# A fused retention and gated feed-forward kernel: a new order for its first sixteen microseconds, and one GpSimd product moved ahead of a hold

## The chip, the core and the metric

The kernel runs on one core of one Trainium2 chip. The metric is the device time of one execution in microseconds (us). Six executions of the kernel before took 226.02 to 227.59 us, with a median of 226.58 us.

A core has five engines with one instruction queue each: PE (TensorE: matrix products, with its weight loads shown apart as PEld), DVE (VectorE), ACT (ScalarE), POOL (GpSimd) and SP (SyncE). Every engine works through its queue in order. An instruction that waits on a semaphore therefore holds up all that stands behind it on the same engine. Transfers are issued by SP, ACT and POOL; the loads that change the type from 32-bit to 16-bit floats are issued by POOL here.

## What is computed

The reference, cut to what matters:

```python
# q, k, v: (4 batches, 8 heads, 768 steps, 64)
for t in range(S):
    state = gamma[None, :, None, None] * state + np.einsum('bhd,bhe->bhde', k[:, :, t], v[:, :, t])
    y[:, :, t] = scale * np.einsum('bhd,bhde->bhe', q[:, :, t], state)
x = y.transpose(0, 2, 1, 3).reshape(B * S, H * D)       # 3072 tokens x 512
gate = 1.0 / (1.0 + np.exp(-(x @ w_gate)))              # w_gate, w_val: 512 x 1536
val = x @ w_val
return gate * val @ w_out                               # w_out: 1536 x 512
```

So there are a retention layer with a decay per head, and after it a feed-forward layer whose gate is a sigmoid.

## The kernel before

**Tiles.** Time is cut in six chunks of 128 steps. A "pair" is one chunk of two batches, so there are twelve pairs: pairs 0 and 1 are the first chunk (batches 0 and 1, then 2 and 3), pairs 2 and 3 the second chunk, and so on to pair 11. Within a pair the retention is done as matrix products: scores of k against q (PE), a product with a table of decays (DVE), then y from the masked scores and v, and from the second chunk on also from a carried state. The feed-forward layer works on a whole chunk t, that is on 512 tokens. Its input is `xT[t]`, with the tokens along the free axis: pair 0 fills columns 0 to 255 of `xT[0]` and pair 1 fills columns 256 to 511.

**The first chunk (pairs 0 and 1)** is done by functions of its own. `first` (L92) loads one batch's part of q, k or v. Batches 0 and 1 of k go as 32-bit floats into `kf`, issued by SP (L101) and by ACT (L102); DVE casts heads 0 to 3 of both batches (L178) and ACT casts heads 4 to 7 (L179). All else is loaded by POOL, in this order: q of batches 0 and 1, k of 2 and 3, q of 2 and 3, v of 0 to 3, and then the weights: `wg` and `wv` in two halves each for the first 256 columns (L119, L120), then whole blocks of 256 columns. Then, for pair i and half g of the heads:

- `first_transpose(i, which, g, eng)` (L340): PE transposes k (which 0) or q (which 1), and `eng` (DVE or ACT) copies the result out of PSUM into `kqT` (L346).
- `first_scores(i, g)` (L348): 16 small products on PE (L355), then two products with the decay table on DVE (L362), which give `st`.
- `first_y(i, engs)` (L364): 32 small products on PE (L372; the first 16 need half 0 of the heads only), then two copies into `xT[0]` (L377), each by the engine named.
- `first_part(w, lo)` (L410): eight products on PE (L415) for 256 columns of the weights and 256 tokens from `lo`. The first four need the first half of the weight block, the others the second half.
- `gate_times_val` (L419): the sigmoid on ACT (L425) and the product of gate and value on DVE (L426).
- `keep_on(n)` (L470): n products of zeros on PE (L473), whose result is not used. They fill time in which PE would stand idle.

`later_constants` (L181) makes three small tables on DVE (L182, L160, L185) and `later_exps` (L188) their exponentials on ACT. The order of all this is the order in which L479 to L533 are written; no scheduler changes it. The feed-forward layer of the first chunk starts at L502 with `first_part` and goes on at L514 with full blocks (L406, `up_part`).

**The later chunks.** The loop at L589 goes over chunks 1 to 5. A chunk's feed-forward work is cut in 20 groups: 12 for the gate and value products (L406), eight for the output product (`down`, L437, products at L442, a copy to `ob` on ACT at L446, and an output transfer on SP at L448 or L451). The table `plan` (L578) says after which group which step of the retention is written out. Its steps:

- `load_next(i)` (L534): POOL issues seven loads for pair i: k in three (L63, L67), q in three, v in one (L57).
- `xbar(i)` (L228): SP issues two transposing transfers, of k and of q, into `kqX` (L231).
- `scale_k(i)` (L234): POOL multiplies k by a table (L236), giving `ks`, which `state(i)` (L290, L295) needs.
- `hold(i)` (L540): POOL copies one column of `kqX` (L541). It waits until the transposing transfer of q of pair i has landed, and so holds back every load that POOL issues after it.
- `block(old, new, st)` (L310): PE does y of pair `old` (`inter`, L270; `intra`, L277), the scores of pair `new` (L254) and the state of pair `st` (L295), with the products on DVE after them (L288, L260, L304).
- `casts(i)` (L306): DVE makes the 16-bit copy `zb` of the state (L308).

In the row of chunk 1, POOL's order before is: product of pair 4, hold on pair 4, the seven loads of pair 6, product of pair 5.

Of the kernel before, what the change touches and what calls it, by code (L numbers as in the profile page):

```python
# [15 lines left out]
def kernel(  # L16
# [12 lines left out]
    nc = tc.nc  # L29
    B, H, S, D = q.shape  # L30
    N_TOK, D_MODEL = out.shape
    D_FF = moe_w_gate.shape[1]
    C = 128
# [39 lines left out]
    wg = wpool.tile([128, KT, D_FF], BF16, name="wg")  # L73
    wv = wpool.tile([128, KT, D_FF], BF16, name="wv")
# [14 lines left out]

    def first(dst, x, b, eng):  # L92
        j = b % 2
        eng.dma_start(out=dst[j * D:(j + 1) * D].rearrange("p h r d -> p h (r d)"),  # L94
                      in_=x[b, :, 0:C, :].rearrange("h (p r) d -> p h (r d)", r=2))

    kf = ld.tile([C, H, 2, D], F32, tag="kf", name="kf", bufs=1)
    k2, q2, v2 = [[ld.tile([C, H, 2, D], BF16, tag=tag, name=tag, bufs=n) for _ in range(2)]
                  for tag, n in (("kn", 6), ("qn", 4), ("vs", 6))]

    first(kf, k, 0, nc.sync)  # L101
    first(kf, k, 1, nc.scalar)  # L102
    nc.scalar.preload_act_table(AX.Exp)
    ahead = const.tile([128, C], F32, name="ahead")
    after = const.tile([128, 3, D], F32, name="after")
# [3 lines left out]
    nc.gpsimd.iota(ahead, pattern=[[-1, C]], base=0, channel_multiplier=1, allow_small_or_imprecise_dtypes=True)  # L109
    nc.gpsimd.iota(after, pattern=[[1, 3], [-2, D]], base=-1, channel_multiplier=2, allow_small_or_imprecise_dtypes=True)  # L110
    first(q2[0], q, 0, nc.gpsimd)
    first(q2[0], q, 1, nc.gpsimd)
    for x, t in ((k, k2[1]), (q, q2[1])):
# [45 lines left out]
    def tab_power(x, lo, n):  # L159
        nc.vector.tensor_tensor(tabs_of[:, :, :, lo:lo + n], x.unsqueeze(1).unsqueeze(1).to_broadcast([128, NP, 2, n]),  # L160
                                nlg.rearrange("s e p -> s p e").unsqueeze(3).to_broadcast([128, NP, 2, n]), op=ALU.mult)
# [19 lines left out]
    def later_constants():  # L181
        nc.vector.tensor_scalar(tok, begin, ahead[:, 0:1], None, op0=ALU.add)  # L182
        tab_power(tok, 0, NT)
        shape = [128, NT, 2, NP]
        nc.vector.tensor_tensor(tabz, lgz.unsqueeze(1).to_broadcast(shape),  # L185
                                begin.unsqueeze(2).unsqueeze(3).to_broadcast(shape), op=ALU.mult)
# [22 lines left out]
    def bank(shape, dt=F32):  # L209
        return pf.tile(shape, dt, tag="ff", name="ff")  # L210

    def half(e):
        return slice(e * D, (e + 1) * D)
# [66 lines left out]
    def new_xT(t):  # L280
        xT[t] = at.tile([128, NP, 512], BF16, tag="xT", name="xT", bufs=2)
# [58 lines left out]
    def first_transpose(i, which, g, eng):  # L340
        tp = bank([128, 2, 2, C], BF16)
        for p in range(2):
            for r in range(2):
                for e in range(2):
                    nc.tensor.transpose(tp[half(e), p, r ^ which], (k2, q2)[which][i][:, 4 * g + 2 * p + e, r, :], ident)
        eng(kq2[i][:, which, 2 * g:2 * g + 2], tp)  # L346

    def first_scores(i, g):  # L348
        t = kq2[i]
        s = [bank([128, 2, 2, C]) for _ in range(2)]  # L350
        for p in range(2):
            for r in range(2):
                for j in range(2):
                    for e in range(2):
                        nc.tensor.matmul(s[e][half(j), p, r].rearrange("s (o p) -> s o p", o=2),  # L355
                                         t[half(e), 0, 2 * g + p, r, half(j)], t[half(e), 1, 2 * g + p, :, half(j)],
                                         start=True, stop=True)
        for e in range(2):
            st0[i, g, e] = at.tile([128, 2, 2, C], BF16, tag=f"st{e}", name=f"st{e}", bufs=4)
            d = decay[:, g, e]  # L360
            d = bass.AP(d.tensor, d.offset, [d.ap[0], d.ap[1], (D, 2), (1, C)])
            nc.vector.tensor_tensor(st0[i, g, e], s[e], d, op=ALU.mult)  # L362

    def first_y(i, engs):  # L364
        if 0 not in xT:
            new_xT(0)
        ys = [bank([128, NP, C]) for _ in range(2)]
        for p in range(NP):
            for r in range(2):
                for j in range(2):  # L370
                    for e in range(2):
                        nc.tensor.matmul(ys[j][half(e), p, :], v2[i][half(j), 2 * p + e, r, :],  # L372
                                         st0[i, p // 2, e][half(j), p % 2, r, :],
                                         start=(p == 0 and r == 0), stop=(r == 1), skip_group_check=True)
        for j in range(2):
            c = (2 * i + j) * C
            engs[j](xT[0][:, :, c:c + C], ys[j])  # L377
# [32 lines left out]
    def first_part(w, lo):  # L410
        u = bank([128, 2, 256])
        for k0 in (0, 2):
            for n1 in range(2):
                for kk in range(k0, k0 + 2):
                    nc.tensor.matmul(u[:, n1], w[:, kk, n1 * 128:(n1 + 1) * 128], xT[0][:, kk, lo:lo + 256],  # L415
                                     start=(kk == 0 and n1 == 0), stop=(kk == KT - 1), skip_group_check=True)
        return u.rearrange("p i n -> p (i n)")

    def gate_times_val(t, n1s, lo, hi, ps):  # L419
        n = hi - lo  # L420
        if t not in hT:
            hT[t] = ffn.tile([128, NFF, 512], BF16, tag="hT", name="hT", bufs=2)
        gs = ffn.tile([128, 512], F32, tag="gs", name="gs")
        g = gs[:, :len(n1s) * n]
        nc.scalar.activation(g, ps[0], AX.Sigmoid)  # L425
        nc.vector.tensor_tensor(hT[t][:, n1s[0]:n1s[-1] + 1, lo:hi], g.rearrange("p (i n) -> p i n", n=n),  # L426
                                ps[1].rearrange("p (i n) -> p i n", n=n), op=ALU.mult)
# [42 lines left out]
    def keep_on(n):  # L470
        u = bank([128, 512])
        for _ in range(n):
            nc.tensor.matmul(u, zero[:, :128], zero, start=True, stop=True)  # L473
# [2 lines left out]

    act, dve = nc.scalar.copy, nc.vector.tensor_copy

    keep_on(11)  # L479
    first_transpose(0, 0, 0, dve)  # L480
    first_transpose(0, 0, 1, act)
    keep_on(1)
    first_transpose(0, 1, 0, dve)
    first_transpose(0, 1, 1, act)
    nc.scalar.activation(taby, taby, AX.Exp, bias=lsc)
    keep_on(1)
    first_scores(0, 0)
    first_scores(0, 1)
    later_constants()
    keep_on(1)  # L490
    first_transpose(1, 0, 0, act)
    first_transpose(1, 0, 1, act)
    keep_on(2)
    first_transpose(1, 1, 0, act)
    first_transpose(1, 1, 1, act)
    keep_on(2)
    first_scores(1, 0)
    first_y(0, (act, act))
    first_scores(1, 1)
    later_exps()  # L500
    keep_on(3)
    gate0 = first_part(wg, 0)  # L502
    first_y(1, (dve, act))
    nc.scalar.preload_act_table(AX.Sigmoid)
    gate_times_val(0, (0, 1), 0, 256, (gate0, first_part(wv, 0)))
    gate_times_val(0, (0, 1), 256, 512, (first_part(wg, 256), first_part(wv, 256)))
    for h in range(2):
        first_scaled(0, h, kf)
    load_gate_val(3)
# [59 lines left out]
    for j in range(2):  # L569
# [6 lines left out]


    plan = {  # L578
        1: [(2, block, None, 3), (4, block, 3, None, 3), (4, xbar, 4), (4, scale_k, 4), (4, hold, 4), (4, load_next, 6),
            (5, casts, 3), (7, xbar, 5), (7, scale_k, 5), (11, block, None, 4, 4), (12, casts, 4), (12, xbar, 6), (12, scale_k, 6),  # L580
            (12, hold, 6), (12, load_next, 7), (14, block, 4, 5, 5), (16, casts, 5), (18, block, 5, 6, 6), (19, casts, 6)],
        2: [(0, xbar, 7), (0, scale_k, 7), (0, hold, 7), (0, load_next, 8), (8, block, 6, 7, 7), (10, casts, 7), (10, xbar, 8),
            (10, scale_k, 8), (10, hold, 8), (10, load_next, 9), (17, block, 7, 8, 8), (19, casts, 8)],
# [47 lines left out]
```

## Time and profile before

| what | value |
|---|---|
| median of six executions | 226.58 us |
| the profiled execution | 226.49 us |
| its span (first to last instruction) | 224.7 us |
| PE busy | 218.9 us (97% of the span) |
| DVE / ACT / POOL busy | 113.2 / 69.8 / 103.8 us |
| dummy products `keep_on` (L473) | 21 |
| first full-width product (L406) starts | 18.41 us |
| last product, then the end of the span | 221.5 us, 224.7 us |

Times in the text are microseconds from the start of the span. A line of the timeline gives the start, the duration, the engine with its line in the kernel, the operation with output and inputs, the number of instructions merged, and in brackets how long the engine stood idle before and what ended that. In the chain of waits a line gives start, duration and the piece of work.

### The profile page before, as it was taken

The numbers are of one execution on the slowest core, as the hardware profiler recorded it, in microseconds if no ns is written. First come the engines' busy times: TensorE is split into PE (matmuls) and PEld (weight loads), VectorE is DVE, ScalarE is ACT, GpSimd is POOL, SyncE is SP. The second block draws the span as 40 slices with busy tenths as digits, with TensorE's granted clock in tenths as the row PEclk, the third lists the DMA queues.
The fourth block names the chain that finished last, engine by engine and source line by source line (L and its number), as shares of the span: only waits on it lengthen the run. The fifth ranks groups of instructions, "written<-read, shape, count | busy, mean of one in ns | idle before, by whom it ended". The sixth has DMA issues, their size and how long they took to land.

```text
span 224.7 us, 4941 instructions
## 1 busy us (share of the span) xinstructions
PE 218.9 (97%) x2061; PEld 117.4 (52%) x2061; DVE 113.2 (50%) x202; ACT 69.8 (31%) x117; POOL 103.8 (46%) x129
## 2 busy tenths in 40 slices
PE   7989999999999999999999999999999999999994
PEld 2555444558888455445445445445445444444443
DVE  8774652264964786846807435906434802333301
ACT  6664333233233112332222332321332322333221
POOL 8999979825993959339195082460000000000000
PEclk9999999999999999999999999999999999999999
DMA  6999999999999999939999689699600012100022
GB/s 125 179 193 197 196 189 187 156 164 170 110 140 132 179 227 129 155 51 115 121 98 183 144 52 152 45 133 139 140 0 3 0 47 96 47 1 0 3 93 93
DMA packets 99702, 25.75 MB, mean 115 GB/s; under 512 B 87648, under 2 KB 96736, under 8 KB 99680
## 3 DMA queue, kind: packets, MB, share of 16 engines
q0 software_dynamic: 75808, 13.90, 76.3%
q1 hardware_dynamic: 23200, 11.21, 24.0%
q10 hardware_dynamic: 672, 0.33, 0.5%
q8 instruction: 16, 0.26, 0.4%
q14 instruction: 6, 0.05, 0.1%
HBM read 28.31 MB, written 6.29 MB: 154 GB/s over the span
## 4 chain that ended last, share of the span: by engine, by line
PE 77%; DMA 11%; POOL 8%; SPq 1%; issue 0%; ACT 0%; DVE 0%; POOLq 0%
PE ff L406 45%; PE ff L442 24%; DMA qn<-in_q_dram 4%; DMA kqX<-qn 3%; DMA wv<-in_moe_w_val_dram 3%; PE ff L277 2%; PE ff L254 2%; DMA kqX<-kn 1%; SPq L451 1%; POOL kn L67 1%; POOL qn L94 1%; PE ff L415 1%; POOL vs L94 1%; PE ff L459 1%; PE ff L270 1%; POOL qn L67 1%
## 5 line engine op out<-in xcount | busy, mean ns | idle before, releaser
L426 DVE TENSOR_TENSOR hT<-gs,ff 128x512 bf16<-128x512 f32 x72 | 49.0, 686 | 58.9 <-PE ff L406 56.9
L406 PE MATMUL ff<-xT,wg 128*128 128x512 bf16 (+1 forms) x328 | 71.8, 348 | 0.0
L406 PE MATMUL ff<-xT,wv 128*128 128x512 bf16 (+1 forms) x328 | 71.7, 348 | 0.0
L425 ACT ACTIVATE gs<-ff 128x512 f32<-128x512 f32 x72 | 42.9, 597 | 82.4 <-PE ff L406 80.2
L442 PE MATMUL ff<-wo,hT 128*128 128x512 bf16 x276 | 62.1, 380 | 0.0
L406 PEld LDWEIGHTS <-wv 128*128 128x128 bf16 x328 | 32.0, 98 | 28.5
L406 PEld LDWEIGHTS <-wg 128*128 128x128 bf16 x328 | 31.5, 98 | 27.9
L442 PEld LDWEIGHTS <-hT 128*128 128x128 bf16 x276 | 26.2, 98 | 30.7
L446 ACT COPY ob<-ff 128x512 f32<-128x512 f32 x23 | 13.5, 585 | 58.6 <-PE ff L442 58.5
L288 DVE TENSOR_TENSOR xT<-ff,taby 128x512 bf16<-128x512 f32 x20 | 12.9, 686 | 30.5 <-PE ff L277 30.5
L260 DVE TENSOR_TENSOR st<-ff,maskk 128x512 bf16<-128x512 f32 x40 | 24.8, 681 | 6.4 <-PE ff L254 6.4
L541 POOL COPY held<-kqX 128x1 bf16<-128x1 bf16 x7 | 1.3, 187 | 41.2 <-DMA kqX<-qn 34.0
L236 POOL TENSOR_TENSOR ks<-kn,tabsk 128x1024 bf16<-128x1024 bf16 x8 | 15.6, 1968 | 0.2 <-DMA kn<-in_k_dram 0.2
L67 POOL DMA_DIRECT2D qn<-in_q_dram x20 | 15.5, 806 | 0.0
L67 POOL DMA_DIRECT2D kn<-in_k_dram x20 | 15.2, 780 | 0.0
L57 POOL DMA_DIRECT2D vs<-in_v_dram x10 | 12.1, 1213 | 0.6 <-DMA wo<-in_moe_w_out_dram 0.5
L63 POOL DMA_DIRECT2D kn<-in_k_dram x10 | 9.3, 925 | 1.8 <-issue 1.7
L63 POOL DMA_DIRECT2D qn<-in_q_dram x10 | 9.3, 929 | 0.0
L473 PE MATMUL ff<-zero 128*128 128x512 bf16 x21 | 8.1, 515 | 1.2 <-DVE zero L141 1.2
L308 DVE TENSOR_TENSOR zb<-za,tabz 128x512 bf16<-128x512 f32 x10 | 8.9, 901 | 0.2
L277 PE MATMUL ff<-st,vs 128*64 128x128 bf16 x160 | 6.4, 222 | 0.0
L79 POOL DMA_DIRECT2D wg<-in_moe_w_gate_dram x7 | 6.0, 871 | 0.0
(80 smaller groups left out, 116.4 us busy)
## 6 DMA issues: line engine op xcount, KB each, us to landing
out_dram<-ob SPq DMA_DIRECT2D x19, 256.0 KB, 2.9
vs<-in_v_dram POOLq DMA_DIRECT2D x10, 256.0 KB, 7.5
qn<-in_q_dram POOLq DMA_DIRECT2D x14, 128.0 KB, 4.9
kn<-in_k_dram POOLq DMA_DIRECT2D x12, 128.0 KB, 4.3
wo<-in_moe_w_out_dram POOLq DMA_DIRECT2D x4, 384.0 KB, 7.0
wg<-in_moe_w_gate_dram POOLq DMA_DIRECT2D x5, 256.0 KB, 7.0
wv<-in_moe_w_val_dram POOLq DMA_DIRECT2D x5, 256.0 KB, 7.5
kn<-in_k_dram POOLq DMA_DIRECT2D x20, 64.0 KB, 4.0
```

What stands on the lines that cost most here:

```text
L57: nc.gpsimd.dma_start(out=vs[i], in_=v[2 * h:2 * h + 2, :, t * C:(t + 1) * C, :].rearrange("b h s d -> s (b h) d"))
L63: nc.gpsimd.dma_start(out=tiles[i][:, 0:H], in_=src[0])
L67: nc.gpsimd.dma_start(out=dst[:, e], in_=pairs[:, 1 - e])
L236: nc.gpsimd.tensor_tensor(ks[i], kn[i], tabsk[:, i // 2].rearrange("s j h -> s (j h)").unsqueeze(2) .to_broadcast([C, 2 * H, D]), op=ALU.mult)
L260: nc.vector.tensor_tensor(st[i, j], sc[i, j][e], maskk[:, e ^ j], op=ALU.mult)
L277: nc.tensor.matmul(y[i, j][half(e), p, :], vs[i][:, j * H + 2 * p + e, :], st[:, p, :], start=False, stop=True, skip_group_check=True)
L288: nc.vector.tensor_tensor(xT[t][:, :, c:c + C], y[i, j], taby, op=ALU.mult)
L406: nc.tensor.matmul(u[:, i * n:(i + 1) * n], w[:, kk, n1 * 128:(n1 + 1) * 128], xT[t][:, kk, lo:hi], start=(kk == 0), stop=(kk == KT - 1))
L425: nc.scalar.activation(g, ps[0], AX.Sigmoid)
L426: nc.vector.tensor_tensor(hT[t][:, n1s[0]:n1s[-1] + 1, lo:hi], g.rearrange("p (i n) -> p i n", n=n), ps[1].rearrange("p (i n) -> p i n", n ...
L442: nc.tensor.matmul(o, hT[t][:, n1, b * C:(b + 1) * C], wo[:, n1, :], start=(n1 == 0), stop=(n1 == NFF - 1))
L446: nc.scalar.copy(ob, o)
```

## The change

It has four parts.

1. **The first k.** The two loads of `kf`, one by SP and one by ACT with all eight heads of one batch each, become four: SP loads heads 0 to 3 of batch 0 and then of batch 1, ACT heads 4 to 7 of both. What DVE casts then comes from SP's queue alone and what ACT casts from ACT's alone.
2. **The order of the first chunk.** `later_constants` goes from behind the scores of pair 0 to the place right behind DVE's cast of k. Pair 1's k is transposed between the two score groups of pair 0. Its q is copied out of PSUM by DVE (half 0) and ACT (half 1), before by ACT alone. `first_y(0)` goes ahead of the scores of pair 1. Three `keep_on` products fewer are issued (18, before 21).
3. **The first feed-forward products.** The gate product of tokens 256 to 511 (`gate1`, which needs pair 1's y) is issued ahead of the value product of tokens 0 to 255. Before it came behind it.
4. **Pair 5's product.** In the row of chunk 1 of the plan, `scale_k(5)` goes from behind `xbar(5)` at group 7 to group 4, ahead of `hold(4)` and of the loads of pair 6.

```diff
-    def first(dst, x, b, eng):
+    def first(dst, x, b, eng, hs=slice(0, H)):
         j = b % 2
-        eng.dma_start(out=dst[j * D:(j + 1) * D].rearrange("p h r d -> p h (r d)"),
-                      in_=x[b, :, 0:C, :].rearrange("h (p r) d -> p h (r d)", r=2))
+        eng.dma_start(out=dst[j * D:(j + 1) * D, hs].rearrange("p h r d -> p h (r d)"),
+                      in_=x[b, hs, 0:C, :].rearrange("h (p r) d -> p h (r d)", r=2))
...
-    first(kf, k, 0, nc.sync)
-    first(kf, k, 1, nc.scalar)
+    for b in range(2):
+        first(kf, k, b, nc.sync, slice(0, 4))
+        first(kf, k, b, nc.scalar, slice(4, 8))
...
+    later_constants()
     keep_on(11)
     first_transpose(0, 0, 0, dve)
     first_transpose(0, 0, 1, act)
-    keep_on(1)
     first_transpose(0, 1, 0, dve)
     first_transpose(0, 1, 1, act)
     nc.scalar.activation(taby, taby, AX.Exp, bias=lsc)
     keep_on(1)
     first_scores(0, 0)
-    first_scores(0, 1)
-    later_constants()
-    keep_on(1)
     first_transpose(1, 0, 0, act)
     first_transpose(1, 0, 1, act)
+    first_scores(0, 1)
     keep_on(2)
-    first_transpose(1, 1, 0, act)
+    first_transpose(1, 1, 0, dve)
     first_transpose(1, 1, 1, act)
-    keep_on(2)
+    keep_on(1)
+    first_y(0, (act, act))
     first_scores(1, 0)
-    first_y(0, (act, act))
     first_scores(1, 1)
     later_exps()
     keep_on(3)
     gate0 = first_part(wg, 0)
     first_y(1, (dve, act))
     nc.scalar.preload_act_table(AX.Sigmoid)
+    gate1 = first_part(wg, 256)
     gate_times_val(0, (0, 1), 0, 256, (gate0, first_part(wv, 0)))
-    gate_times_val(0, (0, 1), 256, 512, (first_part(wg, 256), first_part(wv, 256)))
+    gate_times_val(0, (0, 1), 256, 512, (gate1, first_part(wv, 256)))
...
-        1: [(2, block, None, 3), (4, block, 3, None, 3), (4, xbar, 4), (4, scale_k, 4), (4, hold, 4), (4, load_next, 6),
-            (5, casts, 3), (7, xbar, 5), (7, scale_k, 5), (11, block, None, 4, 4), (12, casts, 4), (12, xbar, 6), (12, scale_k, 6),
+        1: [(2, block, None, 3), (4, block, 3, None, 3), (4, xbar, 4), (4, scale_k, 4), (4, scale_k, 5), (4, hold, 4),
+            (4, load_next, 6), (5, casts, 3), (7, xbar, 5), (11, block, None, 4, 4), (12, casts, 4), (12, xbar, 6), (12, scale_k, 6),
```

The lines that the prediction names are those of the kernel before.

## The prediction

> **What bounds the kernel now.** I read the page first: PE is busy for 218.9 of 224.7 us, so the question is where PE stands still or does work that nobody needs. The waits of PE, in total, times and longest, list all of it:
>
> ```profile
> PE ff L473 <- DVE zero L141: 1.2, 1, 1.2
> PE ff L345 <- DVE kn L178: 0.5, 1, 0.5
> PE ff L415 <- DMA wv<-in_moe_w_val_dram: 0.4, 1, 0.4
> PE ff L254 <- DMA kqX<-qn: 0.2, 1, 0.2
> PE ff L415 <- ACT xT L377: 0.2, 1, 0.2
> ```
>
> All but the fourth lie in the first 16 us. The chain of waits says the same with places:
>
> ```profile
> 9.62 6.06 DMA wv<-in_moe_w_val_dram
> 15.68 0.05 issue
> 15.72 2.85 PE ff L415 x24
> 18.57 6.91 PE ff L406 x32
> ...
> 71.68 6.42 DMA kqX<-qn
> 78.10 0.14 issue
> 78.24 0.64 PE ff L254 x32
> ```
>
> From 15.72 us on, PE runs to the end with one stop, 0.23 us at 78.24. So the whole effect is (1) how far the start of the full-width products (L406, now 18.41) moves, and (2) that stop. Everything earlier counts only through (1). The timeline of that place:
>
> ```profile
> 12.20 2.48 DVE L362 TENSOR_TENSOR st<-ff,decay 128x512 bf16<-128x512 f32 x4
> ...
> 13.71 1.03 PE L415 MATMUL ff<-xT,wg 128*128 128x256 bf16 x8 [0.18 <-ACT xT L377]
> ...
> 14.68 0.64 PE L372 MATMUL ff<-st,vs 64*64 64x128 bf16 x32
> 15.35 0.69 DVE L377 CAST xT<-ff 128x512 bf16<-128x512 f32 x1 [0.68 <-PE ff L372]
> 15.39 0.58 ACT L377 CAST xT<-ff 128x512 bf16<-128x512 f32 x1 [1.45 <-PE ff L372]
> 15.72 0.33 PEld L415 LDWEIGHTS <-wv 128*128 128x128 bf16 x4 [0.57 <-DMA wv<-in_moe_w_val_dram]
> 15.72 1.10 PE L415 MATMUL ff<-xT,wv 128*128 128x256 bf16 x8 [0.41 <-DMA wv<-in_moe_w_val_dram]
> ```
>
> What to see: the value product starts at 15.72, when its weights land, **before** pair 1's xT is ready (16.04, the end of the DVE copy). The weights, not the retention, set the start of the stream.
>
> **What the Trainium skill says.** (a) "DMA: Bandwidth & Descriptors", Issuing engines are not separate DMA queues: transfers of all issuing engines run on the same 16 DMA engines, and several issuers save only issue time. So four halves of k should land about when two wholes did. The trace fits in part: two equal loads, issued together, landed after 5.2 us (SP) and 3.9 us (ACT). (b) "SBUF — State Buffer", Who interferes with whom: some DVE operations from SBUF to SBUF share ports with GpSimd, and the later one waits for the whole instruction of the other. The trace agrees: L182, six elements wide, took 0.56 us and ended at 11.92, just where a load issue of POOL ended (11.01 for 0.91). (c) "TensorE: Matmul & The Clock Gate", What's actually happening: an idle PE falls to half its clock, over windows of about 3.4 us. The trace agrees in that the first eleven dummies took 4.87 us, 0.44 each, and a product as wide later takes 0.22.
>
> **The change, part by part.**
>
> *k in halves.* DVE's cast (L178) starts at 6.06: its queue is full until 5.97 and SP's load landed at 0.74 + 5.2 = 5.94. An earlier landing gives at most 0.1. A later one is possible: each issue now takes 0.73 to 0.78, a half load something between half of that and all of it, so the last half could land up to 0.7 later, or a little earlier. I take nothing. ACT's second issue delays its table load (1.50) by under 0.8, hidden, as the decay tables are wanted at 8.7 and were done at 4.98.
>
> *Scores of pair 0.* `later_constants` now stands between DVE's cast and its copy of k. From L182's start to the next product it cost 12.20 - 11.36 = 0.84, or 0.36 without the port wait. From 6.47 this gives 6.83 to 7.31 for the k copy, now 7.06; I take 7.31, since POOL issues the v loads there. The dummy between the transposes goes, so q's start at 7.17 rather than 7.49 (q's second load: 2.06 + 5.0 = 7.1). The q copy followed by 0.46, so 7.63, or 7.69 behind the k copy; it takes 0.42, and the scores start at 8.17 instead of 8.43. The products on DVE follow by 0.52 and take 2.48: they end at 11.17 instead of 11.43. Pair 1's k transposes at 8.55 find their load landed (3.54 + 4.8 = 8.35), take 0.57, and are hidden under DVE's products.
>
> *Pair 1.* Here the 0.26 is given back. The q copy is queued behind the four products on DVE: 11.10 to 11.52. `first_y(0)`, now ahead of the scores, needs v of batch 1 (6.21 + 5.0 = 11.2) and runs 0.44: 11.25 to 11.70. So the scores start at 11.70 (11.69 before), and DVE's products at 12.1 to 12.2 (12.20), ending by 14.7 as before. The 0.84 of constants that left this place had been standing beside the wait for the same scores.
>
> *Gate 0 and y of pair 1.* `gate0` can start at 13.45, when its first weights land, not 13.71. But its last four products need the second half, issued at 8.90 with 5.2 to landing: 14.10, which is when those weight loads started before. So it ends at about 14.6 as before, `first_y(1)` starts at 14.68, and xT is complete at 16.04. Only the second half of `first_y(1)` needs DVE's last product, so DVE may be 0.2 late for nothing.
>
> *Gate 1 ahead of value 0.* Now PE waits for xT: 16.04 + 0.06 = 16.10, and all three parts stand behind it. They took 0.94, 0.88 and 0.87 (the first with a wait for the second half of wv, landed by 16.21). After: 16.10 + 3 x 0.875 = 18.73, against 18.41. **+0.32 us.** The three dummies removed (0.22 each) stood in waits: nothing.
>
> *Pair 5's product.* POOL before:
>
> ```profile
> 65.31 2.04 POOL L236 TENSOR_TENSOR ks<-kn,tabsk 128x1024 bf16<-128x1024 bf16 x1
> 70.71 0.19 POOL L541 COPY held<-kqX 128x1 bf16<-128x1 bf16 x1 [3.36 <-DMA kqX<-qn]
> 71.17 0.93 POOL L63 DMA_DIRECT2D kn<-in_k_dram  x1 [0.28 <-issue]
> ...
> 77.10 3.83 POOL L236 TENSOR_TENSOR ks<-kn,tabsk 128x1024 bf16<-128x1024 bf16 x2
> ```
>
> The moved product waits for pair 5's k, which SP's transpose found landed at 69.47, and takes 1.92: until about 71.4. The hold and the seven loads of pair 6 stand behind it and start 0.7 later. The transposing transfer of pair 5's q, issued at 71.68, then meets fewer of them in a stretch where the DMA engines are full. 0.7 us of less competition against a stop of 0.23: the stop should go. Bounds: nothing, or 0.23; I take **-0.20**. With it gone the state product at 79.28 would have been next late (its `ks` was ready at 79.0), and that is now ready at 71.4. The loads of pair 6 end 0.7 later; their transposes landed at 83.47 and PE wants them at 85.16, so 1.7 of slack becomes 1.0.
>
> **Sum.** +0.32 - 0.20 = +0.12. The profiled execution took 226.49 (span 224.7 and 1.8 around it), so 226.61; the median of the six is 0.09 above it: **226.7 us**. About 0.3% (0.7 us) is what a measurement of this kernel can tell from no change.
>
> **Rivals.**
>
> *A: as above,* 226.7, own range 226.3 to 227.1 (the stop stays: 226.9; DVE's k copy not delayed: no change, since v sets `first_y(0)`). 0.50.
>
> *B: the gate fills the wait for wv,* as its place suggests. That needs xT of pair 1 before 15.7. For it: only landings hold `gate0` and `first_y(0)`, and k in smaller pieces could free the DMA engines some tenths earlier, for all loads behind. If every landing came 0.4 earlier, `first_y(1)` would start at 14.28, `gate1` at 15.70, L406 at 18.33: -0.08 - 0.20 gives 226.3. If xT came a full 0.8 earlier: -0.5 - 0.2 gives 225.9. Against it: POOL's issues stay back to back at the same times. 0.25, of which 0.15 is beyond 0.3%.
>
> *C: the clock falls,* the slower case. PE now stands idle from 15.2 to 16.1, after gaps before 11.25, before 13.45 and near 14.0, with three dummies fewer. If that tips a window of (c), the products behind it run at half speed for one 3.4 us window: +1.7, so 228.4. It decides once the idle share of such a window passes a limit that no trace here shows. Against it: the stretch before had a similar pattern and stayed at full speed. 0.08.
>
> *D: k lands late.* From a cast over 0.3 late on (the slack at v and in `first_y(1)`), the delay passes on; at 0.7 late, +0.4: 227.1. 0.10.
>
> *E: the loads of pair 6 are late.* From 1.0 of further delay PE stops at 85.2; the spread of such landings between 45 and 90 us (3.1 to 9.1 us) allows another 0.8: 227.5. 0.07.
>
> **Numbers.** Beyond -0.3%: 0.15, out of B. Beyond +0.3%: C, E and the ends of A and D, 0.20. Within: 0.65. The range 226.0 to 227.3 leaves out C, half of E and the end of B, under 2 in 10.
>
> **What would show it.** In the profile after: scores of pair 0 near 8.2; `gate0` in two pieces, from 13.45 and 14.1; an idle PE before `gate1` that ends with xT near 16.1 and no wait for wv; L406 near 18.7; the hold near 71.5 and no stop at 78.2. An L406 before 18.2 would make it wrong, and so would slow 128x512 products behind 18 us, or a new wait after 80 us.

## The result and the profile after

The changed kernel takes 227.53 us, the median of 28 executions (lowest 226.66). The kernel before, run beside it, takes 226.77 us (63 executions). The ratio is 1.003, with a 95% interval of 1.0016 to 1.0045: **slower by 0.3%**, some 0.7 us. Executions in a slower state, with a lower granted clock (the share of full speed that PE was given), and one of 1278 us are left out of the ratio. The forecast was 226.7 us, +0.12 and so no change that can be told; the time lies 0.2 us above the end of its range.

The profiled execution took 226.81 us with a span of 225.0 us; before it was 226.49 and 224.7. Between L103 and the order of the first scores, line numbers are one higher after the change (L407 is what L406 was); the hold stays at L541. The same waits of PE, in total, times and longest:

```profile
PE ff L346 <- DVE kn L179: 1.6, 1, 1.6
...
PE ff L416 <- DVE xT L378: 0.8, 1, 0.8
PE ff L416 <- DMA wg<-in_moe_w_gate_dram: 0.3, 1, 0.3
PE ff L373 <- DMA vs<-in_v_dram: 0.2, 1, 0.2
```

The wait for wv and the one for `kqX` (pair 5's scores) are gone. In their place stand the wait for the first cast of k, 1.6 us instead of 0.5, the wait for xT, and short ones for the gate weights of `gate0` and for v. The chain of waits in the head:

```profile
9.17 5.49 DMA wg<-in_moe_w_gate_dram
...
16.67 2.79 PE ff L416 x24
19.47 6.91 PE ff L407 x32
```

It no longer runs through wv but through the second half of the gate weights of `gate0`, pair 1's products and xT. The 24 products behind xT are the three parts in a row. The last line answers to `18.57 6.91 PE ff L406 x32`: **0.90 us later**. The timeline of the head gives the exact starts:

```profile
0.74 1.65 SPq L94 DMA_DIRECT2D kf<-in_k_dram  x2
...
6.65 0.59 DVE L179 CAST kn<-kf 128x512 bf16<-128x512 f32 x1 [0.67 <-DMA kf<-in_k_dram]
7.16 0.22 DVE L183 TENSOR_SCALAR tok<-begin,ahead 128x6 f32<-128x6 f32 x1
...
14.03 1.29 PE L416 MATMUL ff<-xT,wg 128*128 128x256 bf16 x8 [0.31 <-DMA wg<-in_moe_w_gate_dram]
15.25 0.64 PE L373 MATMUL ff<-st,vs 64*64 64x128 bf16 x32
...
16.67 1.05 PE L416 MATMUL ff<-xT,wg 128*128 128x256 bf16 x8 [0.78 <-DVE xT L378]
...
19.30 1.89 PE L407 MATMUL ff<-xT,wg 128*128 128x512 bf16 x8
```

Read it from the bottom. L407 starts at 19.30, L406 started at 18.41: **+0.89**. From `gate1` to there it is 19.30 - 16.67 = 2.63, the three parts of 0.875 of the forecast. But `gate1` starts 0.57 later than forecast (16.10), as does `first_y(1)` before it (15.25, forecast 14.68), and at the top the cast of k starts 0.59 later than before. The timeline of the kernel before, for that cast and its load:

```profile
0.74 0.78 SPq L94 DMA_DIRECT2D kf<-in_k_dram  x1
...
6.06 0.49 DVE L178 CAST kn<-kf 128x512 bf16<-128x512 f32 x1
```

One load was issued in 0.78 us; two halves take 1.65. So a half load costs as much issue time as a whole one, and the second half is issued not at 0.74 but at about 1.57.

What this does to the transfers is in the view of the DMA engines, for 0 to 12 us in 40 slices of 0.3 us: the busy share of the 16 engines in tenths, and the GB/s that they moved. First the kernel before, then the changed one:

```profile
DMA  0000000246699999999999999999999999999999
GB/s 0 0 0 0 0 0 0 65 96 116 189 299 343 328 221 196 180 179 176 181 175 181 178 177 181 174 184 174 181 176 179 178 180 177 179 178 178 178 180 184
```

```profile
DMA  0000000189957689999999999999999999999999
GB/s 0 0 0 0 0 0 0 43 227 290 306 72 62 98 131 212 234 244 219 190 173 180 179 178 179 178 173 181 176 180 177 178 180 175 180 176 182 177 178 181
```

Before, the whole loads keep 299 to 343 GB/s going from 3.3 to 4.2 us. After, the first halves are through by 3.3 and there is a **hole**: 72, 62 and 98 GB/s from there to 4.2 us. From about 6 us on both move some 178 GB/s with all engines busy, the loads of POOL, and the hole is not made up: adding the slices, 497 KB were moved by 4.5 us before and 369 KB after; by 12 us it is 1842 and 1767 KB. The 75 KB still missing are 0.42 us of work at 178 GB/s.

Not every load is late by that much. The two halves of the gate weights land 0.57 and 0.61 later than before, those of the value weights 0.24 and 0.08. The gate weights' second half is issued at 9.17 instead of 8.92 and lands at 14.66 instead of 14.05. It is issued later because in this program a load on POOL waits for the landing of the load eight before it (below, the rule of eight): in the changed kernel, ten loads in a row, from the third load of v on, are issued 0.28 or 0.29 us after that landing. For the two gate loads it is that of pair 1's k, which landed 5.3 us after issue instead of 4.8.

The time of issue does not explain the hole alone. The view of the tile `kf` gives the time from issue to landing of the four half loads:

```profile
DMA to landing us min/median/max: 3.0/4.1/5.0
```

The first halves landed 3.0 and 3.5 us after their issue. The second halves were issued by 1.57; as quick as the first, they would have landed by 5.1, ahead of the 5.96 of the whole load. But they took 4.8 and 5.0. Loads of POOL moved beside them: 42 KB from 3.3 to 4.5 us, where it was 5 KB before. Whether that is what slowed the second halves is not shown.

At pair 5, the timeline of PE after the change:

```profile
78.48 0.42 PE L271 MATMUL ff<-kqX,zb 64*64 64x128 bf16 x16
78.73 0.62 PE L255 MATMUL ff<-kqX 64*64 64x128 bf16 x32
...
80.10 5.35 PE L443 MATMUL ff<-wo,hT 128*128 128x512 bf16 x24
```

The same place in the kernel before:

```profile
77.59 0.42 PE L270 MATMUL ff<-kqX,zb 64*64 64x128 bf16 x16
...
79.63 5.35 PE L442 MATMUL ff<-wo,hT 128*128 128x512 bf16 x24
```

From L271 to L443 it is 80.10 - 78.48 = 1.62 us; before it was 79.63 - 77.59 = 2.04. The stop is gone, and 0.42 come back of the 0.89. What remains, +0.47, is still there at the last block of products (L459 at 218.68 before, L460 at 219.15 after); the span shows 0.3 of it, as the tail behind that block was shorter.

### The profile page after: what moved, and what is told of

Its sections match the earlier page's. It is cut to its first block, busy times and chain, and to the rows that moved or that the text cites. A ratio compares the mean times of both kernels' runs of the same rounds, so it can differ in the third digit from the quotient of the medians.

```text
span 225.0 us, 4940 instructions
## 1 busy us (share of the span) xinstructions
PE 217.7 (97%) x2058; PEld 117.2 (52%) x2058; DVE 113.6 (51%) x203; ACT 69.1 (31%) x116; POOL 103.8 (46%) x129
## 4 chain that ended last, share of the span: by engine, by line
PE 92%; POOL 4%; DMA 2%; DVE 0%; issue 0%; POOLq 0%
PE ff L407 54%; PE ff L443 27%; PE ff L278 3%; DMA wg<-in_moe_w_gate_dram 2%; PE ff L255 2%; PE ff L271 2%; PE ff L416 2%; POOL qn L94 1%; POOL vs L94 1%; PE ff L460 1%; PE ff L296 1%; POOL kn L94 1%; PE ff L226 0%; POOL wg L79 0%; DVE xT L378 0%; PE ff L391 0%
## 5 line engine op out<-in xcount | busy, mean ns | idle before, releaser
L407 PE MATMUL ff<-xT,wg 128*128 128x512 bf16 (+1 forms) x328 | 71.7, 348 | 0.0
L407 PE MATMUL ff<-xT,wv 128*128 128x512 bf16 (+1 forms) x328 | 71.7, 348 | 0.0
L443 PE MATMUL ff<-wo,hT 128*128 128x512 bf16 x276 | 62.1, 380 | 0.0
L407 PEld LDWEIGHTS <-wv 128*128 128x128 bf16 x328 | 32.0, 98 | 28.5
L407 PEld LDWEIGHTS <-wg 128*128 128x128 bf16 x328 | 31.6, 98 | 27.9
L443 PEld LDWEIGHTS <-hT 128*128 128x128 bf16 x276 | 26.2, 98 | 30.7
L541 POOL COPY held<-kqX 128x1 bf16<-128x1 bf16 x7 | 1.3, 188 | 38.4 <-DMA kqX<-qn 31.0
L67 POOL DMA_DIRECT2D kn<-in_k_dram x20 | 15.2, 778 | 0.0
L474 PE MATMUL ff<-zero 128*128 128x512 bf16 x18 | 6.7, 512 | 1.2 <-DVE zero L142 1.2
L363 DVE TENSOR_TENSOR st<-ff,decay 128x512 bf16<-128x512 f32 x8 | 5.0, 684 | 1.3 <-PE ff L356 1.3
```

Source lines behind the costliest of these rows:

```text
L67: nc.gpsimd.dma_start(out=dst[:, e], in_=pairs[:, 1 - e])
L407: nc.tensor.matmul(u[:, i * n:(i + 1) * n], w[:, kk, n1 * 128:(n1 + 1) * 128], xT[t][:, kk, lo:hi], start=(kk == 0), stop=(kk == KT - 1))
L443: nc.tensor.matmul(o, hT[t][:, n1, b * C:(b + 1) * C], wo[:, n1, :], start=(n1 == 0), stop=(n1 == NFF - 1))
```

## The experiments

The theory, formed on these views: **the halves leave the DMA engines short of work**, which costs about 0.57 us, and `gate1` ahead of the value product costs 0.32 as forecast. The rivals: the clock falls in the head; the loads of pair 6 come late behind the moved product, and PE stops there; the new order of the first scores is to blame. Every experiment leaves the computation whole. Times are compared with runs of the kernel before on the same chip: medians of 226.54 (`after_again`, `e_halves`, `e_whole_k`, `e_gate_late`), 226.72 (`e_product`, `e_no_product`, `e_order_product`, `e_gate_first`), 226.82 (`e_order`, `e_order_product_2`, `e_quarters`, `e_warm`) and 226.56 us (`e_product_mid`, `e_warm_2`, `e_dummies_before`, `after_third`). The expectations stand as they were written, each before its run; some count on what a later run refuted.

### The change again, and its parts undone or alone

**after_again**, the changed kernel without an edit:

> The changed kernel once more, for a second trace and for its own scatter. Theory S (supply): the four half loads of k land later than the two whole ones and push every load of POOL behind them back by 0.3 to 0.6 us; with the gate product ahead of the value product this puts the first full-width product near 19.3 us (18.4 before), and the stop at 78 us is gone (0.4 us back), so about +0.5 us, ratio 1.002. Theory O (order): the new order of DVE's and PE's work in the first chunk is what costs, and the loads only show it. Both expect the same here; a trace with its first full-width product away from 19.3 by over 0.3 would say that the loads' landing varies from run to run.

227.60 us, ratio 1.0046 (1.0024 to 1.0068): the loss is there again. But its profiled execution took 229.88 us, three more than the first. Two lines of its timeline of PE:

```profile
7.67 1.06 PE L346 MATMUL ff<-ident,kn 128*64 128x128 bf16 x16 [1.60 <-DVE kn L179]
...
88.67 0.64 PE L255 MATMUL ff<-kqX 64*64 64x128 bf16 x32 [1.30 <-DMA kqX<-qn]
```

The first transposes ran at half speed (1.06 instead of 0.64), L407 started only at 20.48, 1.2 past the expected 19.3, and there is a stop of 1.3 at pair 6. One trace is thus not enough: below, each place is read in all traces.

**e_halves**, the kernel before with the four half loads alone:

```diff
-    first(kf, k, 0, nc.sync)
-    first(kf, k, 1, nc.scalar)
+    for b in range(2):
+        first(kf, k, b, nc.sync, slice(0, 4))
+        first(kf, k, b, nc.scalar, slice(4, 8))
```

> The kernel before with the first k in four half loads and nothing else. S: DVE's cast of k starts at 6.6 us instead of 6.06, the second half of the first gate weights lands near 14.7 instead of 14.1, pair 1's xT is complete near 16.6, the value product starts near 15.95, and the first full-width product near 18.6: +0.2 us, ratio 1.001. O: the loads are not what costs, the first full-width product stays at 18.4, ratio 1.000.

227.96 us, ratio 1.0066 (1.004 to 1.0092): alone, the halves cost as much as the whole change or more, and more than the 1.001 expected. The timeline of PE says why:

```profile
7.29 0.67 PE L346 MATMUL ff<-ident,kn 128*64 128x128 bf16 x16 [2.01 <-DVE kn L179]
...
8.43 1.06 PE L346 MATMUL ff<-ident,qn 128*64 128x128 bf16 x16
```

PE stands idle for 2.0 us until the cast at 6.74, and the next sixteen transposes take 1.06: the granted clock is 0.64 from 7.3 to 9.0 us, 0.50 from there to 10.8 and 1.00 from 12.0 on. In the order of before, the chain from k's second half to the full-width products (here at 19.83) has no slack left. The cast is 0.68 late here, but pair 1's scores start 1.89 later than before (13.58, before 11.69), so the larger part of that delay arose in the stretch at half speed. In the times it doesn't show: the three executions with a mean clock of 0.992 took 227.65 to 228.1 us, the three at 0.998 or more 227.18, 228.16 and 229.31.

**e_whole_k**, the changed kernel with k in two whole loads again:

```diff
-    for b in range(2):
-        first(kf, k, b, nc.sync, slice(0, 4))
-        first(kf, k, b, nc.scalar, slice(4, 8))
+    first(kf, k, 0, nc.sync)
+    first(kf, k, 1, nc.scalar)
```

> The changed kernel with the two whole loads of k as before. S: cast at 6.06, second half of the gate weights at 14.1, the first full-width product at 18.73 as first forecast, no stop at 78 us: -0.1 us against before, ratio 0.9995, and 0.6 us less than the changed kernel. O: the first full-width product stays above 19.1, ratio 1.001 to 1.002.

227.08 us, ratio 1.0024 (1.0008 to 1.0041); full-width products at 19.15. This is what rival O expected, and not S: in this trace the whole loads were late too, with the cast at 6.55. Against `after_again` half of the loss is gone, against the first measurement (1.003) a fifth; the intervals overlap, so this pair doesn't prove it.

**e_gate_late**, the changed kernel with the second gate product behind the value product again:

```diff
-    gate1 = first_part(wg, 256)
     gate_times_val(0, (0, 1), 0, 256, (gate0, first_part(wv, 0)))
-    gate_times_val(0, (0, 1), 256, 512, (gate1, first_part(wv, 256)))
+    gate_times_val(0, (0, 1), 256, 512, (first_part(wg, 256), first_part(wv, 256)))
```

> The changed kernel with the gate product of tokens 256 to 511 behind the value product again. S: the value product starts near 15.95, when its weights land, the gate product near 16.85, the first full-width product near 18.6 instead of 19.3: ratio 0.999 against before, 0.7 us less than the changed kernel. A rival, that the place of the gate product is indifferent because xT of pair 1 is late in either order: first full-width product still near 19.2, ratio 1.002.

226.96 us, ratio 1.0033 (1.0014 to 1.0052). The timeline of PE:

```profile
16.33 1.05 PE L416 MATMUL ff<-xT,wv 128*128 128x256 bf16 x8 [0.56 <-DMA wv<-in_moe_w_val_dram]
```

With the gate product behind, PE waits for wv again, and wv too lands late: at 16.3 instead of 15.7. L407 starts at 18.96, 0.34 before the changed kernel's, as forecast for this step, and 0.55 after the 18.41 of before. The expectation had 18.6 and 0.999: wv landed 0.4 later here than in the first trace of the changed kernel. Over all traces its first half lands at 15.3 to 16.4 with halves of k and at 15.2 to 15.9 with whole loads, so this wait differs from run to run. In time, the step undone gives no gain that can be told.

**e_gate_first**, the kernel before with `gate1` ahead of the value product (the last hunk turned round), and **e_order**, the kernel before with the order from `later_constants()` down to `later_exps()` alone:

> The kernel before with the gate product of tokens 256 to 511 ahead of the value product and nothing else. By the forecast's own step: PE waits for xT of pair 1 instead of wv, first full-width product 0.3 us later than with the value product first, ratio 1.0014. If xT is as early as the value weights in most executions: ratio 1.000.

> The kernel before with the new order of the first chunk alone (part 2), k whole, the value product first, pair 5's product in its old place. S: cast at 6.0 to 6.2, first full-width product at 18.1 to 18.5 since the weights' landing sets it in either order, stops at pair 5 as before, ratio 0.999 to 1.001. O (the new order costs): first full-width product at 18.8 or later, ratio 1.002.

`e_gate_first`: 226.83 us, 1.0008 (0.9991 to 1.0025), full-width products at 18.83. `e_order`: 226.77 us, 0.9995 (0.9974 to 1.0017), at 18.81, because the second half of its gate weights landed only at 15.02 in that trace. The order costs nothing that can be measured; the 0.3 of the gate product shows in the trace but is as large as what the times can tell.

**e_quarters**, the kernel before with k in eight quarter loads, a dose test of the theory:

```diff
+    for b in range(2):
+        for h in (0, 2):
+            first(kf, k, b, nc.sync, slice(h, h + 2))
+            first(kf, k, b, nc.scalar, slice(4 + h, 6 + h))
```

> The kernel before with the first k in eight quarter loads, four on SP and four on ACT: the suspected cost once more and doubled. I (issue time: each further load on a queue costs SP about 0.8 us whatever its size): last issue near 3.2 us, cast of k at 8.2 us instead of 6.06 (halves: 6.7 to 7.2), first full-width product at 20 or later, ratio 1.008 or more. B (bytes and competition on the DMA engines): the same bytes land no later than as halves, cast near 6.8, ratio near that of the halves, 1.006.

229.89 us, ratio **1.0139** (1.0107 to 1.0171). From the tile view of `kf` (durations of one issue in ns: least, median, most; then first and last start; last, the time to landing), and the timeline:

```profile
L94 SPq DMA_DIRECT2D kf<-in_k_dram x4: 615/705/818, 0.7 to 3.1; - x4
...
DMA to landing us min/median/max: 2.5/4.1/5.7
```

```profile
8.89 1.44 POOL L79 DMA_DIRECT2D wg<-in_moe_w_gate_dram  x2 [0.55 <-DMA kn<-in_k_dram]
8.90 0.43 DVE L180 CAST kn<-kf 128x512 bf16<-128x512 f32 x1 [2.93 <-DMA kf<-in_k_dram]
```

A quarter load (64 KB) costs 0.62 to 0.82 us of issue, as a whole one of 256 KB costs 0.78. The fourth is issued at 3.11, and the cast starts at 8.90; the expectation from issue time had 3.2 and 8.2. Here too the later pieces are slower: the first quarters land 2.5 and 2.7 us after issue, the last ones 5.4 and 5.7. POOL's first gate load stands 0.55 us on the landing of k, as the rule of eight says. By 4.5 us 308 KB had been moved. Five of the six executions show a mean clock of 0.985 to 0.993, so the clock is part of this number; the one at 1.000 took 229.44 us.

**All traces together.** What the edits share can be read across the 18 traces:

| k in | traces | KB moved by 4.5 us | by 12 us | cast of k starts | first gate load issued |
|---|---|---|---|---|---|
| whole loads | 9 | 490 to 527 | 1835 to 1865 | 5.96 to 6.55 | 8.21 to 8.55, median 8.22 |
| halves | 8 | 364 to 396 | 1736 to 1784 | 6.60 to 7.19 | 8.39 to 8.77, median 8.50 |
| quarters | 1 | 308 | 1723 | 8.90 | 8.89 |

Bytes and casts don't overlap, the casts by a margin of only 0.05. The start of the full-width products, as a median over traces (`e_halves` and `e_quarters`, in which the cast decides, are left out; in four traces a record of the first product is missing, and its start is set 0.22 earlier, one product):

| | value product first | `gate1` first |
|---|---|---|
| whole loads | 18.47 (7 traces, 18.09 to 18.81) | 18.83, 19.15 |
| halves | 18.96 (1 trace) | 19.46 (6 traces, 19.26 to 20.48) |

In these few traces either edit moves it by about 0.5, and the two add up to 0.99.

The times of four versions that differ in these two edits alone say which parts cost. All have the new order and pair 5's product as changed. With whole loads and the value product first the ratio is 0.9995 and 1.0005 (`e_order_product` and its repetition, below); with halves added 1.0033 (`e_gate_late`); with `gate1` first added 1.0024 (`e_whole_k`); with both 1.003 and 1.0046. Only both undone takes the loss away. How much of it belongs to each is not told by the times, whose intervals overlap.

### Pair 5's product

**e_product**, the kernel before with the moved product alone; **e_no_product**, the changed kernel without it:

```diff
-        1: [..., (4, scale_k, 4), (4, hold, 4), (4, load_next, 6),
-            (5, casts, 3), (7, xbar, 5), (7, scale_k, 5), ...
+        1: [..., (4, scale_k, 4), (4, scale_k, 5), (4, hold, 4),
+            (4, load_next, 6), (5, casts, 3), (7, xbar, 5), ...
```

> The kernel before with pair 5's product ahead of the hold and nothing else. P (the product pays): no stop at the scores of pair 5, and the transposed q of pair 6 still in time with about 1 us left, so -0.4 us, ratio 0.998. L (the loads behind the hold pay for it): the loads of pair 6 start 0.7 to 1.2 us later, and where their transposes take as long as in the second trace of the changed kernel (14.4 us from the first load to the landing, 12.3 before) PE stops for up to 1.5 us at the scores of pair 6, so ratio 1.000 to 1.003. Its first 40 us are those of the kernel before and give a second trace of them: if the cast of k starts at 6.06 again, whole loads land early as a rule; if near 6.5, the trace on which the forecast was built was a lucky one.

> The changed kernel with pair 5's product behind the loads of pair 6 again (halves, order and gate as changed). P: the stop at the scores of pair 5 is back, so 0.4 us more than the changed kernel, ratio about 1.006. L: the stop at pair 5 is back but the one at pair 6, which only some executions have, is gone; ratio as the changed kernel or below, 1.002 to 1.004.

`e_product`: 226.51 us, 0.9996 (0.9978 to 1.0015). `e_no_product`: 227.58 us, 1.0039 (1.0018 to 1.0061), the same as the changed kernel. So this part gives nothing on average. The trace of `e_no_product` has no stop at pair 5, against what both its expectations said. The timeline of PE in `e_product`:

```profile
77.79 0.42 PE L270 MATMUL ff<-kqX,zb 64*64 64x128 bf16 x16
78.03 0.62 PE L254 MATMUL ff<-kqX 64*64 64x128 bf16 x32
...
86.02 0.64 PE L254 MATMUL ff<-kqX 64*64 64x128 bf16 x32 [0.92 <-DMA kqX<-qn]
```

No stop at pair 5, but one at pair 6 (L270 there starts at 84.69, so the scores come 1.33 later, 1.08 more than the 0.25 of an undisturbed trace). Taking as stop the time from L270's start to the scores less that 0.25, over the traces: with the moved product (10) the mean is 0.10 at pair 5 and 0.36 at pair 6, where three show over 1 us; without it (7) it is 0.34 and 0.12. The sums are equal, 0.47 and 0.47. **With the edit the time lost lies mostly at pair 6, without it mostly at pair 5.** That the edit moves the stop is an indication only: three of the seven traces without it have no stop at either place, and one of them (`e_gate_first`) has 0.87 at pair 6.

**e_order_product**, the order and the product in the kernel before, and the same again as **e_order_product_2**:

> The order of the first chunk and pair 5's product as changed, k in two whole loads and the gate product behind the value product as before. S (late k and the gate product are what costs): first full-width product at 18.4 to 18.7, no stop at 78 us, ratio 0.998 to 1.000. O (the new order costs too): first full-width product at 19.0 or later, ratio 1.002.

> The new order and pair 5's product, with whole loads of k and the value product first, once more: its first interval held both a gain and no change. S: cast of k near 6.0, first full-width product at 18.1 to 18.5, no stop at the scores of pair 5, ratio 0.997 to 0.999. Rival: its one trace was a lucky run, ratio 1.000 to 1.002.

The first run gave 226.12 us in the median and 225.71 in the profiled execution, which looked like a better kernel; but the ratio was 0.9995 (0.9968 to 1.0022), and the repetition gave 227.03 us, 1.0005 (0.9986 to 1.0025). It is scatter: no version here beats the kernel before.

**e_product_mid**, the kernel before with pair 5's product between pair 6's k and q loads and its v loads:

```diff
-        ..., (4, hold, 4), (4, load_next, 6), (5, casts, 3), (7, xbar, 5), (7, scale_k, 5), ...
+        ..., (4, hold, 4), (4, load_kq, 6), (4, scale_k, 5), (4, load_v, 6), (5, casts, 3), (7, xbar, 5), ...
```

> The kernel before with pair 5's product behind the loads of k and q of pair 6 and ahead of that of v; the hold and the first six loads keep their times. M (the stop at pair 5 goes because the loads of pair 6 start later and leave the transposing transfer alone): the stop of 0.3 to 0.5 us at the scores of pair 5 stays, ratio 1.000. K (it goes because the product is early): no stop, ratio 0.998.

227.76 us, 1.0033 (1.0001 to 1.0065); no stop at pair 5 and 0.84 at pair 6, though pair 6's k and q loads were not behind the product. It is a miss for both expectations: what sets the landing of pair 6's transposes isn't told apart by it and stays open.

### The clock

**e_warm** and **e_warm_2**, the changed kernel with 15 dummies instead of 11 ahead of the first transposes, so that PE waits less before the cast; **e_dummies_before**, the same in the kernel before; and **after_third**, the changed kernel once more with a single execution:

```diff
-    keep_on(11)
+    keep_on(15)
```

> The changed kernel with 15 dummy products ahead of the first transposes instead of 11, so that PE stands idle for about 0.7 us less while it waits for k. C (the clock falls in that idle time in some executions and is part of the cost): no execution with a mean clock below 0.995 (four of 27 before), median 0.1 to 0.3 us below the changed kernel, ratio to before 1.002. If the clock is no part of it: ratio as the changed kernel, 1.003 to 1.005.

> The changed kernel with 15 dummies, a second trace. D: the dummies end at 7.3 to 7.6, past k's cast, and the transposes start up to 0.3 later than with 11. That alone would not explain 1.3 us; if the trace shows later stops of PE (pair 5 or 6) of about 1 us, these are the rest; if it shows products at half speed behind 8 us, the clock is.

> The kernel before with 15 dummies instead of 11 ahead of the first transposes. D (the dummies themselves delay the transposes): they end between 6.5 us (if the clock rises early) and 7.6 us (if all run at 0.43 us each), later than k's cast (6.5), so the first transposes start up to 1 us later and the ratio is 1.002 to 1.005. N (the dummies are harmless): they end before the cast, ratio 1.000.

> The changed kernel, a third trace. Cast of k at 6.6 to 7.2, first full-width product at 19.3 or later, by what S and the earlier traces showed; a cast near 6.1 would say that the halves are not what delays k.

`e_warm`: 228.91 us, 1.0087 (1.0057 to 1.0118). `e_warm_2`: 227.91 us, 1.0064 (1.0033 to 1.0094), with no execution below a mean clock of 0.998. `e_dummies_before`: 226.88 us, 1.0004 (0.9989 to 1.0019). `after_third`: 228.28 us, with a stop of 1.09 at pair 6. If the clock made the loss, dummies in the gap would have taken it away; they didn't, and the loss stands at full clock. The clock costs something in single executions (the trace of `e_halves`; 4 of 27 of the changed kernel show a mean of 0.991 or 0.992; five of six of `e_quarters` are below 0.995), but it isn't the cause. Why four more dummies make the changed kernel slower, and not the kernel before, isn't settled.

## Why the prediction was wrong

**What bounds the kernel** was read rightly: PE has no more stops than those listed, and the loss is the later start of the full-width products less the stop at pair 5.

**"k in halves ... I take nothing" is the step that failed.** Its upper bound said it: an issue that costs as much for a half as for a whole, and a last half up to 0.7 later. Measured: the second issue at about 1.57, the cast 0.6 late in the profiled execution and 0.7 late in the medians of the traces, and 0.57 on the start of the full-width products (0.5 in the table). It is the largest piece that the sum of +0.12 lacked. I took nothing because of point (a), that all issuers share the same DMA engines. That statement holds: k's halves and POOL's loads did share them. It does not follow that pieces land when wholes do. Each piece needs an issue of its own, which the same sentence sets apart, and the second halves took 1.5 to 1.7 us longer to land than the first. The Trainium skill, "Perfetto Trace Analysis", section DMA Optimizations, says that splitting may let the task complete sooner where the DMA engines are generally idle. They were at most six tenths busy in the kernel before until 3.3 us, so the case seemed to be that one, and the measurement says the opposite: 1.0066 for halves and 1.0139 for quarters.

**Scores of pair 0**: forecast 8.17, measured 8.67, the 0.59 of the cast and nearly 0.1 given back. The constants did not hold up the copy of k: it followed the start of the transposes by 0.46 as before, as `tok` took 0.22 instead of the 0.56 that I took with the port wait. The load issue of POOL beside it had begun only 0.15 us before `tok`; the last section has what the traces show of this wait. The cheap bound of that step was the right one, though its 0.36 was too small: with `tok` at 0.22 it is 0.84 - 0.34 = 0.50.

**Pair 1, gate 0, y of pair 1**: the structure was right. `first_y(0)` waits for v, `gate0` comes in two pieces and ends with the landing of its second half, and `first_y(1)` hangs on that. Only the landings moved, from the 14.10 forecast to 14.66. The new order also does what it says: with halves, the changed kernel without part 3 (`e_gate_late`, 1.0033) loses half of what halves cost in the old order (`e_halves`, 1.0066). Those intervals overlap, so that is an indication.

**Gate 1 ahead of value 0, +0.32**: right by the traces, 0.34 between `e_gate_late` and the changed kernel, though the table's medians say up to 0.5. By the times it is neither proved nor refuted (`e_gate_first`, 1.0008, with 0.32 us being 0.0014).

**Pair 5's product, -0.20**: right in the profiled execution, where it gave 0.42 instead of 0.20, since the wait shown was shorter than the time lost around it. As an average it was wrong, 0.9996, and this is the second term that failed: the gain of 0.20 in the sum was not there. A stop at pair 6, which rival E had as 0.07 likely, is seen in 3 of 10 traces, and the mean over both places is no smaller than without the edit. That the stop comes from the later loads, as E says, is not shown.

**The rivals.** D had the cause, a late k, but priced it at 0.4 by way of the cast. In the changed order the cast has slack, as `first_y(0)` waits for v behind it (the 0.2 in the waits), and the price is paid by POOL's weight loads, which land late and, by the rule of eight, are issued late. B is refuted: landings came later, not earlier. C was seen in single traces and doesn't explain the loss.

**The sum anew**: 0.32 for the gate and 0.57 for the halves less 0.42 at pair 5 is the +0.47 seen from 80 us on, of which the span shows 0.3. The medians say 0.76. Likely reasons are that the stop at pair 5 isn't always there to be saved and that stops of over 1 us at pair 6 come up in some executions; the runs don't settle it.

## What to carry to other kernels

Before splitting a load, look at what one issue costs and what the DMA engines do meanwhile: here a half cost as much issue time as the whole, the second half was slower to land than the first, the last byte came 0.6 us later (2.8 with quarters), and the loads queued next paid for it. Where a stop on a transfer vanishes, look for one at the next transfer, in several traces and not in one. And a single profiled execution that is 0.3% better is worth a repetition before it is believed.

## What the runs showed of the hardware that was not expected

- The issue of a load of k costs 0.62 to 0.83 us whether it moves 256, 128 or 64 KB.
- After an idle stretch of PE of 2.0 us (`e_halves`, 5.28 to 7.29 us) its products ran at half speed for about 3.5 us. Of two traces of the changed kernel with 1.6 us of idle before the same transposes, the first stayed at full speed, and so did `e_no_product` with 1.76 and `e_whole_k` with 1.86.
- In the second of them, `after_again`, sixteen transposes took 1.06 us instead of 0.64 while the recorded clock was 1.00: the length of the products, not the record alone, shows the speed.
- A DVE product of six columns (`tok`) beside a load issue of POOL: in the 11 traces in which the issue had begun at least 0.19 us earlier, `tok` took 0.41 to 0.59 us and ended within 0.03 us of the issue's end. In the 7 others, where the issue had begun 0.16 us earlier or less, began later or was not there, it took 0.21 to 0.23.
- Of two half loads of k that SP or ACT issued within 0.9 us of each other, the second took 1.5 to 1.7 us longer to land (the changed kernel).
